# Issuing the keys' weight from ScalarE instead of SyncE at the start of a pre-LN linear-attention and feed-forward block

## The chip, the cores and the metric

The kernel runs on one core of one Trainium2 chip. The core has five engines with a queue of instructions each: TensorE (PE, whose weight loads are listed apart as PEld), VectorE (DVE), ScalarE (ACT), GpSimd (POOL) and SyncE (SP), which here only issues DMAs. Each engine takes its instructions in the order in which they stand in its queue. The DMAs are carried out by 16 DMA engines of the core. The metric is the device time in microseconds (us) of one execution.

## The reference

The inputs are bf16: x of 2048 rows by 512 columns, `wqkv` (512 by 1536), `wo` (512 by 512), `w1` (512 by 1792), `w2` (1792 by 512). Cut to what is computed:

```
ln = layernorm(x)
q, k, v = split(ln @ wqkv)                 # 32 heads of 16 columns
phi(t) = where(t > 0, t + 1, exp(t)) + 1e-6
kv = sum over rows of phi(k)^T v           # per head, 16 x 16
z  = sum over rows of phi(k)
o  = (phi(q) @ kv) / (phi(q) . z + 1e-6)
h  = x + o @ wo
out = h + relu(layernorm(h) @ w1) @ w2
```

## The kernel before

The 2048 rows are 16 tiles of 128 rows. Tile t holds, on partition p, row 16p + t, so tiles that follow each other lie side by side in DRAM on a partition: a DMA of one tile moves pieces of 1 KB, one of two tiles pieces of 2 KB, one of four tiles pieces of 4 KB. Four tiles make a chunk of 512 rows, and there are four chunks. All weights stay in SBUF. PSUM is used as eight banks of 512 columns (`bk`).

The work is written as small operations (`op_...`), and the string ORDER lists them in the order in which they are emitted; a word such as `K.0.3.0.2` calls `op_K(0, 3, 0, 2)`. Nothing reorders them afterwards, so ORDER fixes the order on each engine's queue. The waits between engines are semaphores that the framework adds by data dependence. For the DMAs it uses eight semaphores in turn (DMAHW0 to DMAHW7): the ninth DMA of the program waits until the first has landed, and so on.

The beginning of the program, for each tile t:

- `lx.t.n` (L201) loads n tiles of x into `x_nat`; `lk.k.n` (L204 and L206) loads n of the four row blocks of the keys' weight into `wk_sb` (two blocks are 256 KB). Both are issued by SyncE.
- `S.t` (L226, VectorE) takes the row statistics, `A.t` (L227, VectorE) turns them into mean and variance, `R.t.n` (L232 and L233, ScalarE) computes 1/sqrt by a Ln and an Exp, and `N.t` (L251, VectorE) writes the normalised tile into `h_nat`.
- `T.t` (L270, TensorE) transposes the normalised tiles 0 to 3 into PSUM, and `E.t` (L280, ScalarE) copies them out into `lnT`. The tiles from 4 on are transposed by DMA (`X.t`, L291, issued by SyncE).
- `K.t` (L299, TensorE) is the keys' projection of a tile, four matmuls of 512 columns with `wk_sb`. `F.t` (L317) and `U.t` (L320, both ScalarE) take exp and relu of it, `M.t` (L324) and `D.t` (L327, both VectorE) make phi(k) of the two.
- `G.t` (L351, TensorE) adds the tile's product of the normalised rows and phi(k) to the sum over rows, from which kv follows later.
- `table` (L166) loads ScalarE's function table, and `warm` (L215) runs 11 matmuls on zeros before the first data is there.

Behind these come the queries (`Q`, L307), the small products for kv, the division, the attention's output `h` (L494), the second layernorm, and the feed-forward part (`p`, L510, and `f`, L530), which takes the longer half of the time.

VectorE's queue begins, behind four memsets: S.0 S.1 A.0 S.2 A.1 S.3 A.2 N.0 A.3 N.1 N.2 N.3 S.4 S.5 A.4 A.5 S.7 N.5 S.6 M.0 A.7 A.6 D.0. The code of the loads:

```
    def op_lx(t, n):
        nc.sync.dma_start(out=x_nat[:, t : t + n, :], in_=x_v[:, t : t + n, :])

    op_lk = lambda k, n: load_d(wk_sb, wqkv_v[:, :, D : 2 * D], k, n)
```

Of the kernel before, what the change touches and what calls it, by code (L numbers as in the profile page):

```python
# [15 lines left out]


ORDER = """
const masks table lx.0.1 lx.1.1 lx.2.1 S.0 S.1 A.0 S.2 warm.1.6 lx.3.1 A.1 R.0.1 S.3 A.2 R.1.1 warm.9.6 N.0 A.3
N.1 R.2.1 R.3.1 lk.0.2 N.2 N.3 warm.1.6 T.0.2 T.1.7 lx.4.2 T.2.5 lk.2.2 S.4 E.0 S.5 T.3.4 A.4 K.0.3.0.2 E.1  # L20
K.1.0.0.2 lx.6.2 E.2 E.3 A.5 R.4.2 K.0.3.2.2 S.7 F.0.1 N.5 S.6 K.3.7 M.0.1 lx.8.4 K.2.2.0.2 U.0.1 lx.12.4 A.7
A.6 K.1.0.2.2 D.0.1 F.3.1 U.3.1 R.6.2 N.4 K.2.2.2.2 M.3.1 G.0 D.3.1 G.3 F.2.1 F.1.1 N.6 N.7 S.8 S.9 X.5 X.4
M.2.1 A.8 A.9 U.2.1 U.1.1 K.5.1 R.8.2 K.4.0 M.1.1 D.2.1 F.4.2 D.1.1 N.9 U.4.2 N.8 X.7 S.12 X.6 X.9 G.2 K.7.3
S.13 A.12 A.13 G.1 K.6.2 K.9.1 M.4.2 S.10 R.12.2 F.6.2 N.12 D.4.2 S.11 A.10 U.6.2 X.8 lq.0.2 M.6.2 N.13 G.4 X.12
K.8.0 A.11 R.10.2 D.6.2 lv.0.2 X.13 G.5 G.6 N.10 N.11 S.15 S.14 F.8.2 M.8.2 U.8.2 G.7 X.11 A.15 A.14 D.8.2
R.14.2 N.15 K.12.0 N.14 za.2 za.4 X.10 G.9 lq.2.2 lv.2.2 K.13.1 K.11.3 F.12.2 U.12.2 X.15 X.14 l2.10.4 l2.3.4
l1.0.2 K.10.2 G.8 M.12.2 F.10.2 U.10.2 za.6 D.12.2 M.10.2 za.8 D.10.2 Q.0.0.0 Q.0.1.1 qF.0.0.2 qU.0.0.2 za.10
qM.0.0.2 K.15.3 G.12 K.14.2 F.14.2 G.11 Q.0.2.0 Q.0.3.1 qF.0.2.2 G.13 za.12 M.14.2 W.14.2 zf.12 qD.0.0.2
qM.0.2.2 qU.0.2.2 G.10 G.14 z.3.3.14 G.15 z.1.3.14 z.2.3.14 z.0.3.14 qD.0.2.2 zc Q.1.0.2 gA.0.2 gA.2.2 zh dn.0.1
Q.1.1.3 dnl.0 kv.0.4 kv.2.4 kv.1.4 kv.3.4 lo.0.2 lo.2.2 dnx.0.2.2 qF.1.0.2 dnx.0.0.2 Q.1.2.0 rt.2.7 kx qM.1.0.2  # L30
Q.1.3.1 qF.1.2.2 m.0.4 m.1.5 rv.2 qW.1.0.2 qM.1.2.2 Q.3.1.7 m.3.6 Q.2.3.2 l1.2.2 dt.3 mA.0.2 qW.1.2.2 dt.0 dt.1
m.2.5 Q.2.1.4 dn.1.3 mA.2.2 dm.0.0.2 dm.0.2.2 dnl.1 dnx.1.2.2 Q.2.2.1 h.3.6 dnx.1.0.2 h.1.5 hD.3 dt.7 qF.2.2.2
rt.6.3 s.3 dt.4 re.6 h.0.0 hD.1 qU.2.2.2 dt.5 a.3 hD.0 s.1 s.0 qM.2.2.2 a.0 Q.3.0.6 h.2.5 Q.2.0.3 n.3 n.0 a.1
dm.1.0.2 Q.3.2.0 Q.3.3.1 dm.1.2.2 x.0 x.3 hD.2 n.1 s.2 qF.3.0.2 qU.2.0.2 qF.2.0.2 h.5.2 h.6.3 a.2 qU.3.0.2
qF.3.2.2 qM.2.0.2 h.4.7 n.2 qD.2.0.2 t.2.5 qD.2.2.2 hD.5 hD.4 h.7.4 dn.2.6 hD.7 e.2 dnl.2 x.1 hD.6 qM.3.0.2
p.0.0.5 dnx.2.2.2 p.0.13.7 p.0.1.6 p.0.8.2 p.0.11.4 qD.3.0.2 s.4 dnx.2.0.2 p.0.9.3 l2.7.3 dt.10 pA.0.0.2 dt.11
l2.0.3 dt.9 dt.8 p.0.12.6 qM.3.2.2 qW.3.2.2 s.6 pD.0.12.2 p.0.3.1 p.0.2.0 pA.0.8.2 s.7 r.0.4 dn.3.6 p.0.5.3
p.0.4.2 a.7 dm.2.0.2 dnl.3 pA.0.2.2 dnx.3.0.2 dnx.3.2.2 pA.0.4.2 dm.2.2.2 p.0.7.7 h.9.0 h.8.5 p.0.6.6 n.7 s.5
dt.13 dt.12 p.0.10.3 hD.9 hD.8 s.8 a.6 pD.0.6.2 dt.15 a.4 n.6 dt.14 pA.0.10.2 f.1.1.0.7 dm.3.0.2 dm.3.2.2 h.11.0
f.1.1.7.7 h.12.4 fo.1 s.9 h.15.6 h.14.5 h.10.3 f.0.2.0.7 a.8 a.9 a.5 hD.11 n.5 hD.12 x.6 hD.15 f.3.4.0.7 h.13.7  # L40
f.3.4.7.7 x.7 s.12 n.8 n.4 hD.14 f.0.2.7.7 x.4 x.5 p.1.0.6 f.2.5.0.7 s.11 s.14 hD.13 fo.3 fo.0 hD.10 a.11 s.10
n.9 p.1.5.3 p.1.1.7 s.15 a.12 pA.1.0.2 p.1.4.2 f.2.5.7.7 p.1.13.7 p.1.3.1 a.10 n.12 r.4.4 pA.1.4.2 p.1.2.0 n.11
p.1.8.4 fo.2 a.14 a.15 s.13 p.1.12.6 n.10 p.1.7.2 pD.1.2.2 n.14 p.1.6.1 x.11 p.1.9.5 pA.1.6.2 x.10 a.13 n.15 x.9
x.8 pD.1.8.2 fd.3 f.5.3.0.7 f.7.0.0.7 p.1.10.1 fd.1 fd.0 pA.1.12.2 p.1.11.2 pA.1.10.2 p.2.9.7 p.2.11.6 f.7.0.7.7
p.2.10.5 p.2.5.1 f.5.3.7.7 fo.7 pD.2.10.2 p.2.8.6 p.2.4.0 r.8.4 f.4.4.0.7 f.4.4.7.7 fo.5 p.2.0.2 pD.2.8.2
pD.2.4.2 p.2.1.3 x.12 n.13 p.2.3.6 p.2.2.5 fd.2 f.6.0.0.7 x.14 x.13 pA.2.0.2 pA.2.2.2 x.15 fo.4 p.3.3.7 p.3.7.1
p.3.2.6 p.3.9.5 p.3.8.4 f.6.0.7.7 pD.3.2.2 fo.6 pD.3.8.2 fd.4 p.3.11.7 p.3.4.2 p.3.10.6 p.3.5.3 p.3.6.0
pA.3.10.2 fd.7 pA.3.6.2 p.2.7.7 fd.5 fd.6 p.2.6.6 pA.2.6.2 p.3.13.5 pD.3.4.2 p.3.0.1 p.3.1.2 p.2.13.7 p.2.12.6
f.11.3.0.7 p.3.12.4 pA.3.0.2 pA.2.12.2 r.12.4 pD.3.12.2 f.9.6.0.7 f.14.2.0.7 f.10.7.0.7 f.11.3.7.7 f.10.7.7.7
f.9.6.7.7 f.8.1.0.7 f.12.5.0.7 f.8.1.7.7 f.13.0.0.7 f.15.4.0.14.3.1 f.14.2.7.7 fo.9 fo.10 fo.11 fd.10 fd.11 fd.9  # L50
f.12.5.7.7 fo.8 f.13.0.7.7 f.15.3.0.14.0.2 fd.8 fo.14 fo.12 fo.13 fo.15.3.1 fd.12 f.15.1.0.14.2.1 fd.13
fd.15.3.1 fd.14 fo.15.0.2 fd.15.0.2 fo.15.2.1 fd.15.2.1
"""
# [3 lines left out]
def kernel(  # L57
# [144 lines left out]

    def load_d(dst, src, k, n):
        nc.sync.dma_start(out=dst[:, k : k + n, :], in_=src[:, k : k + n, :])  # L204
# [376 lines left out]
```

## Time and profile before

| what | us |
|---|---|
| median of the runs before (170.41 to 173.28) | 170.55 |
| the profiled execution's own time | 170.57 |
| its span in the trace | 168.9 |
| TensorE busy in it | 162.5 |
| VectorE busy | 101.1 |
| ScalarE busy | 67.7 |

The span runs from the first to the last instruction that the trace shows; 1.7 us of the execution lie around it. "Busy" counts a matmul up to its modelled end, so TensorE at 96% isn't TensorE at its peak. In the timelines a row gives the start, the duration, engine, line, operation and what is written from what; a number in square brackets is the engine's idle time before it and what ended that. SPq is SyncE's queue: its rows are the issuing of a DMA, not the transfer.

### The profile page before, as it was taken

What the parts mean: (1) busy time and instruction counts of PE and PEld (TensorE: products, weight loads), DVE (VectorE), ACT (ScalarE), POOL (GpSimd) and SP (SyncE); (2) the same over time, 40 slices, a digit from 0 to 9 for tenths busy, and PEclk for the clock granted to TensorE, in tenths of its full rate; (3) what the DMA queues carried; (4) which work ended last, traced back from release to release, by engine and by line L of the source; (5) the groups of instructions that cost most, each with busy time, mean ns of one, the idle gap of its engine ahead of it and who ended that gap; (6) DMA issues with size and microseconds to landing.
All of it is one profiled execution on the core that took longest, in us unless ns stands there. A gap on an engine that the chain in (4) does not pass through costs nothing.

```text
span 168.9 us, 2311 instructions
## 1 busy us (share of the span) xinstructions
PE 162.5 (96%) x871; PEld 76.1 (45%) x871; DVE 101.1 (60%) x202; ACT 67.7 (40%) x100; POOL 4.7 (3%) x21
## 2 busy tenths in 40 slices
...
GB/s 124 276 240 92 89 178 117 217 385 336 37 64 62 64 157 67 151 62 97 33 64 0 31 36 157 86 4 0 80 76 0 31 4 0 0 0 88 36 35 93
DMA packets 30635, 15.49 MB, mean 92 GB/s; under 512 B 23200, under 2 KB 29600, under 8 KB 30624
## 3 DMA queue, kind: packets, MB, share of 16 engines
...
q8 instruction: 7, 0.11, 0.3%
...
HBM read 7.86 MB, written 2.10 MB: 59 GB/s over the span
## 4 chain that ended last, share of the span: by engine, by line
PE 91%; DMA 3%; SPq 2%; DVE 1%; issue 1%
PE bk L530 29%; PE bk L510 29%; PE bk L351 8%; PE bk L307 8%; PE bk L494 8%; PE bk L299 6%; DMA x_nat<-in_A_x_dram 3%; SPq L201 1%; PE bk L448 1%; PE bk L392 1%; SPq L204 1%; PE bk L404 1%; PE bk L270 0%; DVE st L226 0%; DVE pk_lo L327 0%
## 5 line engine op out<-in xcount | busy, mean ns | idle before, releaser
L530 PE MATMUL bk<-w_sb,at 128*128 128x512 bf16 (+2 forms) x252 | 50.7, 355 | 0.0
L510 PE MATMUL bk<-lnT,w_sb 128*128 128x512 bf16 x224 | 50.5, 379 | 0.0
L516 ACT ACTIVATE at<-bk 128x1024 bf16<-128x1024 f32 x17 | 17.3, 1021 | 55.6 <-PE bk L510 55.6
L530 PEld LDWEIGHTS <-at 128*128 128x128 bf16 x252 | 23.6, 98 | 25.2 <-DVE at L521 0.2
L510 PEld LDWEIGHTS <-w_sb 128*128 128x128 bf16 x224 | 21.8, 98 | 26.0
L538 DVE SCALAR_TENSOR_TENSOR gT<-bk,rstd,h_nat 128x512 bf16<-128x512 f32 (+2 forms) x18 | 12.2, 690 | 31.2 <-PE bk L530 31.2
L521 DVE TENSOR_SCALAR at<-bk 128x1024 bf16<-128x1024 f32 x11 | 13.3, 1220 | 20.7 <-PE bk L510 20.4
L317 ACT ACTIVATE eb<-bk 128x1024 bf16<-128x1024 f32 (+1 forms) x18 | 16.6, 926 | 6.7 <-PE bk L299 4.0
L307 PE MATMUL bk<-lnT,wq_sb 128*128 128x512 bf16 x64 | 15.8, 379 | 0.0
L299 PE MATMUL bk<-wk_sb,lnT 128*128 128x512 bf16 x64 | 15.3, 379 | 0.0
L494 PE MATMUL bk<-m_sb,pqs 128*128 128x512 bf16 x64 | 15.3, 379 | 0.0
L351 PE MATMUL bk<-at,h_nat 128*128 128x512 bf16 x56 | 13.6, 379 | 0.0
L320 ACT ACTIVATE rb<-bk 128x1024 bf16<-128x1024 f32 (+1 forms) x14 | 12.5, 903 | 0.7 <-PE bk L307 0.7
L226 DVE BATCH_NORM_STATS2 st<-x_nat 128x6 f32<-128x512 bf16 x16 | 10.5, 684 | 3.0 <-DMA x_nat<-in_A_x_dram 3.0
L500 DVE TENSOR_TENSOR h_nat<-bk,x_nat 128x512 bf16<-128x512 f32 x16 | 10.6, 681 | 2.4 <-PE bk L494 2.3
L228 DVE BATCH_NORM_STATS2 st<-h_nat 128x6 f32<-128x512 bf16 x16 | 10.8, 685 | 0.1
L351 PEld LDWEIGHTS <-h_nat 128*128 128x128 bf16 x64 | 6.2, 97 | 8.8 <-issue 1.8
L299 PEld LDWEIGHTS <-lnT 128*128 128x128 bf16 x64 | 5.9, 98 | 7.8 <-DMA lnT<-h_nat 1.4
L494 PEld LDWEIGHTS <-pqs 128*128 128x128 bf16 x64 | 6.1, 98 | 7.2 <-DVE pqs L484 0.8
L307 PEld LDWEIGHTS <-wq_sb 128*128 128x128 bf16 x64 | 5.9, 97 | 6.5 <-DMA wq_sb<-in_A_wqkv_dram 0.4
L461 ACT ACTIVATE wk_sb<-ld 128x1024 bf16<-128x1024 f32 x8 | 8.1, 1051 | 0.1
L324 DVE TENSOR_SCALAR eb<-eb 128x1024 bf16<-128x1024 bf16 (+1 forms) x18 | 6.9, 383 | 0.6 <-ACT eb L317 0.6
...
## 6 DMA issues: line engine op xcount, KB each, us to landing
out_dram<-gT SPq DMA_DIRECT2D x15, 128.0 KB, 1.9
...
x_nat<-in_A_x_dram SPq DMA_DIRECT2D x4, 128.0 KB, 2.5
wk_sb<-in_A_wqkv_dram SPq DMA_DIRECT2D x2, 256.0 KB, 4.2
x_nat<-in_A_x_dram SPq DMA_DIRECT2D x2, 256.0 KB, 5.0
```

The lines of the kernel that those rows point to most:

```text
L228: op_s = lambda t: nc.vector.bn_stats(out=st2[:, t, :], in_=h_nat[:, t, :])
L299: nc.tensor.matmul(bk[:, b, :], lhsT=lnT[c][:, kd, j * P : (j + 1) * P], rhs=wk_sb[:, kd, :], start=(kd == 0), stop=(kd == KD - 1),)
L307: nc.tensor.matmul(bk[:, b, :], lhsT=wq_sb[:, kd, j * P : (j + 1) * P], rhs=lnT[c][:, kd, :], start=(kd == 0), stop=(kd == KD - 1),)
L317: nc.scalar.activation(out=buf(eb, kind, i, n), in_=bank(at_bank[kind, i], n), func=ACT.Exp)
L320: nc.scalar.activation(out=buf(rb, kind, i, n), in_=bank(at_bank[kind, i], n), func=ACT.Relu)
L351: nc.tensor.matmul(bk[:, KD + kd, :], lhsT=ln_nat[:, t, kd * P : (kd + 1) * P], rhs=pk(t)[:, 0, :], start=(t == 0), stop=(t == NT - 1),)
L494: nc.tensor.matmul(bk[:, b, :], lhsT=pqs[:, (c * KD + jb) % NQ, j * P : (j + 1) * P], rhs=m_sb[:, jb, :], start=(jb == 0), stop=(jb == KD ...
L510: nc.tensor.matmul(bk[:, b, cols], lhsT=w1_sb[:, kd, f * P : (f + 1) * P], rhs=lnT[c][:, kd, cols], start=(kd == 0), stop=(kd == KD - 1),)
L516: nc.scalar.activation(out=acts[c % 2][:, f : f + n, :], in_=bank(at_bank["p", c, f], n), func=ACT.Relu)
L521: nc.vector.tensor_scalar(out=acts[c % 2][:, f : f + n, :], in0=bank(at_bank["p", c, f], n), scalar1=0.0, scalar2=None, op0=ALU.max,)
L530: nc.tensor.matmul(bk[:, b, 0 : w * P], lhsT=acts[c % 2][:, f, j * P : (j + 1) * P], rhs=w2_sb[:, f, k * P : (k + w) * P], start=(f == 0), ...
L538: nc.vector.scalar_tensor_tensor(out=o_t[:, t % NO, cols], in0=bk[:, at_bank["f", t, k], 0 : w * P], scalar=rstd2[:, t : t + 1], in1=h_nat ...
```

## The change

The two loads of the keys' weight are issued by ScalarE's queue, as its first two instructions, ahead of the table load. SyncE issues only x at the start, and tiles 2 and 3, which were two DMAs of 128 KB, become one of 256 KB. The order of all other operations stays. In ORDER, four words `lx.0.1 lx.1.1 lx.2.1 lx.3.1` become `lx.0.1 lx.1.1 lx.2.2`, the words `lk.0.2` and `lk.2.2` go, `la.0.2 la.2.2` come, and all words `lx` stand at the front.

```diff
 ORDER = """
-const masks table lx.0.1 lx.1.1 lx.2.1 S.0 S.1 A.0 S.2 warm.1.6 lx.3.1 A.1 R.0.1 S.3 A.2 R.1.1 warm.9.6 N.0 A.3
-N.1 R.2.1 R.3.1 lk.0.2 N.2 N.3 warm.1.6 T.0.2 T.1.7 lx.4.2 T.2.5 lk.2.2 S.4 E.0 S.5 T.3.4 A.4 K.0.3.0.2 E.1
...
+const masks la.0.2 la.2.2 table lx.0.1 lx.1.1 lx.2.2 lx.4.2 lx.6.2 lx.8.4 lx.12.4 S.0 S.1 A.0 S.2 warm.1.6 A.1
...
+    def op_la(k, n):
+        nc.scalar.dma_start(out=wk_sb[:, k : k + n, :], in_=wqkv_v[:, k : k + n, D : 2 * D])
```

(A second new function, `op_xa`, would load x by ScalarE; no word of ORDER calls it.)

On SyncE, the start of the queue before, with the semaphores that a row waits for; 128x512 is one tile of x, 128x1024 two, 128x2048 four, and `wk_sb` is the keys' weight:

```order
L201 DMA x_nat<-in_A_x_dram 128x512 x4
L204 DMA wk_sb<-in_A_wqkv_dram 128x2x512
L201 DMA x_nat<-in_A_x_dram 128x1024
L204 DMA wk_sb<-in_A_wqkv_dram 128x2x512
L201 DMA x_nat<-in_A_x_dram 128x1024
L201 DMA x_nat<-in_A_x_dram 128x2048 [waits DMAHW0_49]
L201 DMA x_nat<-in_A_x_dram 128x2048 [waits DMAHW1_49]
L291 DMA_TRANSPOSE lnT_82<-h_nat 128x4x128 [waits DMAHW2_49,DVE_49]
```

The same place now (line numbers behind L204 are 6 higher, since two functions are added):

```order
L201 DMA x_nat<-in_A_x_dram 128x512 x2
L201 DMA x_nat<-in_A_x_dram 128x1024 x3
L201 DMA x_nat<-in_A_x_dram 128x2048
L201 DMA x_nat<-in_A_x_dram 128x2048 [waits DMAHW0_49]
L297 DMA_TRANSPOSE lnT_82<-h_nat 128x4x128 [waits DMAHW1_49,DVE_49]
```

Three instructions are gone from SyncE's queue: the two of the weight, and one by joining tiles 2 and 3. DMAHW0 is now the semaphore of the weight's first half, which is the program's first DMA, so the load of tiles 12 to 15 waits for that, where before it waited for tile 1; the first DMA transpose waits for the weight's second half where it waited for tile 2.

On ScalarE, the start of the queue before, from the branch into the program on:

```order
L576 UNCONDITIONAL_BRANCH [waits barrier_Pool_Activation_PE_DVE_SP_release]
L166 ACT_TABLE_LOAD
L232 ACTIVATE rstd<-mv,eps_73 128x1 [waits DVE_49]
L233 ACTIVATE rstd<-rstd 128x1 [waits Activation_49]
L232 ACTIVATE rstd<-mv,eps_73 128x1 [waits DVE_49]
```

And now:

```order
L582 UNCONDITIONAL_BRANCH [waits barrier_Pool_Activation_PE_DVE_SP_release]
L210 DMA wk_sb<-in_A_wqkv_dram 128x2x512 x2
L166 ACT_TABLE_LOAD
L238 ACTIVATE rstd<-mv,eps_73 128x1 [waits DVE_49]
L239 ACTIVATE rstd<-rstd 128x1 [waits Activation_49]
```

Two DMA issues stand ahead of the table load and wait for nothing. TensorE's, VectorE's and GpSimd's queues hold the same rows in the same order as before.

More of the change, by code (lines that the diff above doesn't have):

```diff
@@ L18 @@
 ORDER = """
-const masks table lx.0.1 lx.1.1 lx.2.1 S.0 S.1 A.0 S.2 warm.1.6 lx.3.1 A.1 R.0.1 S.3 A.2 R.1.1 warm.9.6 N.0 A.3
-N.1 R.2.1 R.3.1 lk.0.2 N.2 N.3 warm.1.6 T.0.2 T.1.7 lx.4.2 T.2.5 lk.2.2 S.4 E.0 S.5 T.3.4 A.4 K.0.3.0.2 E.1
-K.1.0.0.2 lx.6.2 E.2 E.3 A.5 R.4.2 K.0.3.2.2 S.7 F.0.1 N.5 S.6 K.3.7 M.0.1 lx.8.4 K.2.2.0.2 U.0.1 lx.12.4 A.7
-A.6 K.1.0.2.2 D.0.1 F.3.1 U.3.1 R.6.2 N.4 K.2.2.2.2 M.3.1 G.0 D.3.1 G.3 F.2.1 F.1.1 N.6 N.7 S.8 S.9 X.5 X.4
-M.2.1 A.8 A.9 U.2.1 U.1.1 K.5.1 R.8.2 K.4.0 M.1.1 D.2.1 F.4.2 D.1.1 N.9 U.4.2 N.8 X.7 S.12 X.6 X.9 G.2 K.7.3
@@ L24 @@
[L24 to L48, printed above, removed]
@@ L49 @@
-f.11.3.0.7 p.3.12.4 pA.3.0.2 pA.2.12.2 r.12.4 pD.3.12.2 f.9.6.0.7 f.14.2.0.7 f.10.7.0.7 f.11.3.7.7 f.10.7.7.7
-f.9.6.7.7 f.8.1.0.7 f.12.5.0.7 f.8.1.7.7 f.13.0.0.7 f.15.4.0.14.3.1 f.14.2.7.7 fo.9 fo.10 fo.11 fd.10 fd.11 fd.9
+const masks la.0.2 la.2.2 table lx.0.1 lx.1.1 lx.2.2 lx.4.2 lx.6.2 lx.8.4 lx.12.4 S.0 S.1 A.0 S.2 warm.1.6 A.1
+R.0.1 S.3 A.2 R.1.1 warm.9.6 N.0 A.3 N.1 R.2.1 R.3.1 N.2 N.3 warm.1.6 T.0.2 T.1.7 T.2.5 S.4 E.0 S.5 T.3.4 A.4
+K.0.3.0.2 E.1 K.1.0.0.2 E.2 E.3 A.5 R.4.2 K.0.3.2.2 S.7 F.0.1 N.5 S.6 K.3.7 M.0.1 K.2.2.0.2 U.0.1 A.7 A.6
@@ new lines @@
+K.1.0.2.2 D.0.1 F.3.1 U.3.1 R.6.2 N.4 K.2.2.2.2 M.3.1 G.0 D.3.1 G.3 F.2.1 F.1.1 N.6 N.7 S.8 S.9 X.5 X.4 M.2.1
+A.8 A.9 U.2.1 U.1.1 K.5.1 R.8.2 K.4.0 M.1.1 D.2.1 F.4.2 D.1.1 N.9 U.4.2 N.8 X.7 S.12 X.6 X.9 G.2 K.7.3 S.13 A.12
+A.13 G.1 K.6.2 K.9.1 M.4.2 S.10 R.12.2 F.6.2 N.12 D.4.2 S.11 A.10 U.6.2 X.8 lq.0.2 M.6.2 N.13 G.4 X.12 K.8.0
+A.11 R.10.2 D.6.2 lv.0.2 X.13 G.5 G.6 N.10 N.11 S.15 S.14 F.8.2 M.8.2 U.8.2 G.7 X.11 A.15 A.14 D.8.2 R.14.2 N.15
+K.12.0 N.14 za.2 za.4 X.10 G.9 lq.2.2 lv.2.2 K.13.1 K.11.3 F.12.2 U.12.2 X.15 X.14 l2.10.4 l2.3.4 l1.0.2 K.10.2
@@ new lines @@
+G.8 M.12.2 F.10.2 U.10.2 za.6 D.12.2 M.10.2 za.8 D.10.2 Q.0.0.0 Q.0.1.1 qF.0.0.2 qU.0.0.2 za.10 qM.0.0.2 K.15.3
+G.12 K.14.2 F.14.2 G.11 Q.0.2.0 Q.0.3.1 qF.0.2.2 G.13 za.12 M.14.2 W.14.2 zf.12 qD.0.0.2 qM.0.2.2 qU.0.2.2 G.10
+G.14 z.3.3.14 G.15 z.1.3.14 z.2.3.14 z.0.3.14 qD.0.2.2 zc Q.1.0.2 gA.0.2 gA.2.2 zh dn.0.1 Q.1.1.3 dnl.0 kv.0.4
+kv.2.4 kv.1.4 kv.3.4 lo.0.2 lo.2.2 dnx.0.2.2 qF.1.0.2 dnx.0.0.2 Q.1.2.0 rt.2.7 kx qM.1.0.2 Q.1.3.1 qF.1.2.2
+m.0.4 m.1.5 rv.2 qW.1.0.2 qM.1.2.2 Q.3.1.7 m.3.6 Q.2.3.2 l1.2.2 dt.3 mA.0.2 qW.1.2.2 dt.0 dt.1 m.2.5 Q.2.1.4
@@ new lines @@
+dn.1.3 mA.2.2 dm.0.0.2 dm.0.2.2 dnl.1 dnx.1.2.2 Q.2.2.1 h.3.6 dnx.1.0.2 h.1.5 hD.3 dt.7 qF.2.2.2 rt.6.3 s.3 dt.4
+re.6 h.0.0 hD.1 qU.2.2.2 dt.5 a.3 hD.0 s.1 s.0 qM.2.2.2 a.0 Q.3.0.6 h.2.5 Q.2.0.3 n.3 n.0 a.1 dm.1.0.2 Q.3.2.0
+Q.3.3.1 dm.1.2.2 x.0 x.3 hD.2 n.1 s.2 qF.3.0.2 qU.2.0.2 qF.2.0.2 h.5.2 h.6.3 a.2 qU.3.0.2 qF.3.2.2 qM.2.0.2
+h.4.7 n.2 qD.2.0.2 t.2.5 qD.2.2.2 hD.5 hD.4 h.7.4 dn.2.6 hD.7 e.2 dnl.2 x.1 hD.6 qM.3.0.2 p.0.0.5 dnx.2.2.2
+p.0.13.7 p.0.1.6 p.0.8.2 p.0.11.4 qD.3.0.2 s.4 dnx.2.0.2 p.0.9.3 l2.7.3 dt.10 pA.0.0.2 dt.11 l2.0.3 dt.9 dt.8
```

16 lines of the change are left out of this document (added).

## The prediction

> **What bounds the kernel now.** I read the page first (busy shares, then the chain that ended last), then TensorE's waits, then the chain's first 13 us, and last the timelines and transfers there.
>
> ```profile
> span 168.9 us, 2311 instructions
> PE 162.5 (96%) x871; PEld 76.1 (45%) x871; DVE 101.1 (60%) x202; ACT 67.7 (40%) x100; POOL 4.7 (3%) x21
> ...
> PE 91%; DMA 3%; SPq 2%; DVE 1%; issue 1%
> ```
>
> The kernel is TensorE from end to end: 91% of the chain is matmuls. The change touches none of them. What it can touch is the time in which TensorE waits, and TensorE's list of waits has only three entries:
>
> ```profile
> PE bk L215 <- DVE ones L177: 1.3, 1, 1.3
> PE bk L270 <- DVE h_nat L251: 1.2, 1, 1.2
> PE bk L351 <- DVE pk_lo L327: 1.0, 1, 1.0
> ```
>
> The columns are the total, the number of times and the longest. All three lie in the first 13 us: the start, T.0 waiting for N.0, and G.0 waiting for D.0. Behind G.0 TensorE has no wait in the list, so whatever G.0 moves by, the end moves by. The chain shows what set G.0:
>
> ```profile
> 4.12 5.80 DMA x_nat<-in_A_x_dram
> ...
> 9.95 0.04 DVE st L226
> ...
> 10.56 0.40 DVE h_nat L251
> 10.96 0.60 DVE st L226
> ...
> 11.86 0.44 DVE pk_lo L327
> ...
> 12.33 0.81 PE bk L351 x3
> ```
>
> The load of tiles 6 and 7, issued at 4.12, lands at 9.92; S.7 starts at 9.95, and N.5, S.6, M.0 and D.0 follow on VectorE without a break until G.0 at 12.33. VectorE's timeline up to there:
>
> ```profile
> 3.08 1.30 DVE L226 BATCH_NORM_STATS2 st<-x_nat 128x6 f32<-128x512 bf16 x2 [1.86 <-DMA x_nat<-in_A_x_dram]
> ...
> 4.39 0.66 DVE L226 BATCH_NORM_STATS2 st<-x_nat 128x6 f32<-128x512 bf16 x1
> ...
> 5.16 0.69 DVE L226 BATCH_NORM_STATS2 st<-x_nat 128x6 f32<-128x512 bf16 x1
> ...
> 5.85 0.45 DVE L251 TENSOR_SCALAR h_nat<-x_nat,mv,rstd 128x512 bf16<-128x512 bf16 x1
> ...
> 7.32 1.28 DVE L226 BATCH_NORM_STATS2 st<-x_nat 128x6 f32<-128x512 bf16 x2
> 8.51 0.30 DVE L227 BATCH_NORM_AGGREGATE mv<-st 128x2 f32<-128x6 f32 x2
> 9.95 0.69 DVE L226 BATCH_NORM_STATS2 st<-x_nat 128x6 f32<-128x512 bf16 x1 [1.14 <-DMA x_nat<-in_A_x_dram]
> ```
>
> From S.0 at 3.08 on VectorE works through S.1, S.2 (4.39), S.3 (5.16), N.0 (5.85), S.4 and S.5 (7.32), A.4 and A.5 (8.51 to 8.81), and only then stands still for 1.14 us, for tiles 6 and 7. So there is a **cushion of 1.14 us**: VectorE could run 1.14 us late up to 8.81 and G.0 would still start at 12.33.
>
> **What the change does.** SyncE's part of it, as it is now:
>
> ```profile
> 0.80 1.82 SPq L201 DMA_DIRECT2D x_nat<-in_A_x_dram  x4
> 2.66 0.43 SPq L204 DMA_DIRECT2D wk_sb<-in_A_wqkv_dram  x1
> 3.14 0.47 SPq L201 DMA_DIRECT2D x_nat<-in_A_x_dram  x1
> 3.65 0.43 SPq L204 DMA_DIRECT2D wk_sb<-in_A_wqkv_dram  x1
> 4.12 1.42 SPq L201 DMA_DIRECT2D x_nat<-in_A_x_dram  x3
> ```
>
> *Removed:* three issues from SyncE, 0.43 us each and 0.05 between. x is issued at 0.80, 1.26, 1.72 (tiles 2 and 3), 2.2 (4 and 5) and 2.7 (6 and 7) instead of 0.80 to 2.19, 3.14 and 4.12. Tiles 6 and 7 thus go out 1.4 us earlier. That is worth something only if the transfers, not the issuing, have room:
>
> ```profile
> 2.00:4.00 2.00, 2.00 (x6) 0.76 (x5) 0.92 (x2) 0.08 (x1) 1.72 (x7) 1.00 0.98 240
> 4.00:6.00 2.00, 1.16 (x5) 0.29 (x3) 1.97 (x7) 1.03 (x5) 1.65 (x7) 1.00 0.83 227
> 6.00:8.00 2.00, 1.64 (x18) 1.04 (x19) 2.00 (x7) 1.94 (x7) 0.15 (x1) 1.00 1.02 302
> 8.00:10.00 2.00, 2.00 (x11) 0.89 (x10) 0.86 (x5) 1.97 (x6) 0.00 (x0) 1.00 0.92 353
> ```
>
> The last two columns are the mean busy share of the 16 DMA engines and GB/s. From 2 to 10 us the engines are busy 0.83 to 1.02 of the time: they are already full, with one queue feeding them. And what has to pass before tiles 6 and 7 are in is the same in both orders: all of tiles 0 to 7 (1024 KB) and the weight (512 KB). So I expect their landing near 9.9 as before, at most some 0.3 earlier. The earlier issue buys nearly nothing.
>
> *Moved:* the weight's 512 KB. Before, it stood behind tiles 0 to 3; now its issue starts at about 0.8 on ScalarE, beside tile 0. What was landed when, in KB counted from the first DMA, comes from the transfers' view, one row for each DMA (KB, us from issue to landing); the issues are, in this order, tile 3 (2.19), the weight's first half (2.66), tiles 4 and 5 (3.14) and the weight's second half (3.65):
>
> ```profile
> x_nat<-in_A_x_dram SPq DMA_DIRECT2D x1, 128.0 KB, 2.9
> ...
> wk_sb<-in_A_wqkv_dram SPq DMA_DIRECT2D x1, 256.0 KB, 3.9
> ...
> x_nat<-in_A_x_dram SPq DMA_DIRECT2D x1, 256.0 KB, 4.1
> ...
> wk_sb<-in_A_wqkv_dram SPq DMA_DIRECT2D x1, 256.0 KB, 4.6
> ```
>
> Tile 3 landed at 5.1 as KB 512, the first half at 6.6 as KB 768, tiles 4 and 5 at 7.2 as KB 1024, the second half at 8.2 as KB 1280. I use this as a clock for any order of the same transfers. Issue to landing of tiles 2 and 3 under two queues is not in this trace, so it is bounded: not before 5.1 if the weight took no bandwidth from x (KB 512, as now), and 7.2 if all of the weight passes first (KB 1024). Between them I take an estimate: if the DMA engines take turns row by row between the two queues, then when the last of tile 0's 128 rows, tile 1's 128 and the 128 double rows of tiles 2 and 3 is through, 384 of the weight's 512 rows are too: 512 + 384 = KB 896, about **6.9**, midway between 6.6 and 7.2. By the same count tile 0 lands at KB 256 and tile 1 at KB 512 (5.1), so S.0 and S.1 are late as well but done by 5.9, under the wait of S.2.
>
> The Trainium skill, "DMA: Bandwidth & Descriptors", section "Issuing engines are not separate DMA queues", speaks against this change: DMAs that several engines start run on the same 16 DMA engines and interleave, and only issue time on the sequencer is saved. By it the sum stands as taken; were it wrong, the lower bound would hold. No row of this trace shows two queues at once.
>
> *The sum.* S.3 now starts at 5.16 and N.0 at 5.85. S.2 to S.3 is 5.16 - 4.39 = 0.77, some of it the wait for tile 3; S.0 to S.1, where nothing waits, is 1.30 - 0.69 = 0.61; with A.1 between I take 0.7. With S.2 at 6.9, S.3 starts at 7.6. VectorE is thus late by 7.6 - 5.16 = 2.4 us up to A.5, which ends at 11.2, behind the landing of tiles 6 and 7: the wait of 1.14 is gone. S.7, and with it G.0, is late by 2.4 - 1.14 = **1.3 us**. With the bounds 6.6 and 7.2 it is 1.0 and 1.6.
>
> TensorE in that stretch:
>
> ```profile
> 6.36 1.49 PE L270 MATMUL bk<-ident,h_nat 128*128 128x128 bf16 x16 [1.20 <-DVE h_nat L251]
> 7.69 3.62 PE L299 MATMUL bk<-wk_sb,lnT 128*128 128x512 bf16 x16
> ```
>
> The transposes and the K matmuls are late by the whole 2.4 us: K ends at 7.69 + 3.62 + 2.4 = 13.7, and D.0 allows G.0 at 12.33 + 1.3 = 13.6. The two meet; at most 0.1 is added, and since successive matmuls overlap at their ends I count 0.
>
> *Added:* two DMA issues ahead of the table load.
>
> ```profile
> 0.79 1.28 ACT L166 ACT_TABLE_LOAD   x1 [0.79 <-PEq L565]
> 4.50 0.29 ACT L232 ACTIVATE rstd<-mv,eps 128x1 f32<-128x1 f32 x1 [2.43 <-DVE mv L227]
> ```
>
> At SyncE's 0.43 + 0.05 each, the load ends at 3.0 instead of 2.07, and R.0 isn't due before 4.50, later still now: ScalarE's idle 2.43 us hides it, and the cost is 0 (if the cover went, 0.95). *Landing of the weight:* K.0, due at 7.69 + 2.4, needs its first half, there by about 7.2 at the latest by the clock above: hidden. *The new semaphore waits:* the load of tiles 12 to 15 now waits for the weight's first half, until up to 7.2 instead of 5.1; ahead of it 512 KB of tiles 8 to 11 keep the DMA engines fed meanwhile, so nothing. The first transpose waits for the second half, long landed when N.5 allows it.
>
> So 170.57 (the profiled execution, span 168.9 and 1.7 around it, equal to the median of 170.55 within 0.02) + 1.3 = **171.9 us**, 0.8% slower.
>
> **Rivals.**
>
> *Neutral: x keeps its place.* If tile 0 to 3's loads hold their lead (ScalarE's DMAs start moving later, or its queue gets less), VectorE is late by up to 1.14 us only, and tiles 6 and 7 decide as they do now: 170.3 to 170.9. For it: SyncE's 1.72 for tiles 2 and 3 isn't later than now. Against: the weight is issued as early as tile 0, and the engines are full.
>
> *Faster: two queues move more.* The engines move 240 GB/s at 2 to 4 us and 353 at 8 to 10, at like busy shares, so the early rate, on 1 KB rows, isn't their ceiling. If two queues bring the late rate forward, tiles 2 and 3 come at 4.5 to 5, tiles 6 and 7 before 8.81, and the third of TensorE's waits, 1.0 us, falls: 169.5 to 170.3, no better, as the 1.2 us wait for N.0 stays. Against: the busy share.
>
> *Slower still: TensorE falls back to its slow pace.*
>
> ```profile
> 1.25 3.91 PE L215 MATMUL bk<-m_sb 128*128 128x512 bf16 x11 [1.25 <-DVE ones L177]
> ...
> 2.51 0.15 PEld L215 LDWEIGHTS <-m_sb 128*128 128x128 bf16 x1 [0.28 <-issue]
> ...
> 2.93 0.15 PEld L215 LDWEIGHTS <-m_sb 128*128 128x128 bf16 x1 [0.28 <-issue]
> ...
> 4.13 0.53 PEld L215 LDWEIGHTS <-m_sb 128*128 128x128 bf16 x3 [0.19 <-issue]
> ```
>
> The first warm matmuls' weights are loaded 2.93 - 2.51 = 0.42 us apart; from 4.13 on three fit into 0.53, and the K matmuls take 3.62 / 16 = 0.23 each. So TensorE is slow for its first 4.13 - 1.25 = 2.9 us, though the windows give the granted clock as 1.00 there too. The idle between warm and T.0, 1.20 us now, becomes 1.20 + 2.4 = 3.6 us. If that much idle brings the slow pace back, each K matmul costs 0.2 more: 0.8 us for the four or so that fall into the first 2.9 us of work from T.0 on (T itself takes 1.3 of them), 3.2 us for all 16, and G.0 takes all of it, as TensorE and VectorE meet there: 172.7 to 175.1. It decides from an idle that is longer than this trace's 1.2 us, and it passes 2% if over ten of the K matmuls are slow. For it: the slow start. Against: the idle is short, and T's matmuls end it.
>
> The Trainium skill, "TensorE: Matmul & The Clock Gate", section "What's actually happening", has the gate go back to half rate after an idle window of about 3.4 us that runs freely; by it a gap of 3.6 us need not contain a whole window, and the time would be the forecast's or this rival's as the window happens to fall.
>
> **How the numbers follow.** The forecast has 0.58, its own range 171.1 to 172.6 (bounds 6.6 and 7.2, and some 0.4 for the slowest of the 16 engines); neutral 0.15, faster 0.10, slow pace 0.15, and 0.02 for anything else. The range leaves out the faster case and the dearer half of the slow pace: 170.2 to 173.4. Over 2% slower (above 173.96) is the dear third of the slow pace, 0.05; over 2% faster, below 167.1, is out of reach of the 1.0 us wait, 0.01; within 2%, about what a measurement of this kernel can tell from no change, 0.94.
>
> **What would show it.** S.2's row on VectorE with a wait for x of about 1 us and a start near 6.9; tiles 2 and 3 with some 5.2 us from issue to landing; N.0 near 8.3; the idle before T.0 at 3.6; no idle before S.7; G.0 near 13.6; K matmuls still 0.23 each; ScalarE's table load ending near 3.0. I am wrong if S.2 starts before 5.8, if S.7 still waits for x, or if the K matmuls take 0.42 each.

## The result and the profile after

The changed kernel takes 172.38 us (median, 171.37 to 172.74) against 170.55: the ratio is 1.0113, with a 95% interval of 1.0073 to 1.0152. That is 1.1% slower, and inside the forecast range (170.2 to 173.4), 0.5 us above the forecast of 171.9. The profiled execution took 172.74, with a span of 171.0, 2.2 us longer than the span before. Executions over 1.5% above the fastest of their kernel (173.28 and 172.29 of the kernel before, 172.69 of e9_before_warm below) are left out of the ratios. Lines behind L204 are 6 higher now: L226 is L232, L299 is L305, L351 is L357.

TensorE's waits, which had three entries, have two; the columns are the total, the number and the longest:

```profile
PE bk L276 <- DVE h_nat L257: 2.7, 1, 2.7
PE bk L221 <- DVE ones L177: 1.2, 1, 1.2
```

T.0's wait for N.0 has grown from 1.2 to 2.7 us, and the wait of G.0 is gone. VectorE's timeline shows where T.0's wait comes from:

```profile
3.32 0.70 DVE L232 BATCH_NORM_STATS2 st<-x_nat 128x6 f32<-128x512 bf16 x1 [2.10 <-DMA x_nat<-in_A_x_dram]
4.59 0.69 DVE L232 BATCH_NORM_STATS2 st<-x_nat 128x6 f32<-128x512 bf16 x1 [0.57 <-DMA x_nat<-in_A_x_dram]
...
6.76 0.69 DVE L232 BATCH_NORM_STATS2 st<-x_nat 128x6 f32<-128x512 bf16 x1 [1.40 <-DMA x_nat<-in_A_x_dram]
...
8.12 0.38 DVE L257 TENSOR_SCALAR h_nat<-x_nat,mv,rstd 128x512 bf16<-128x512 bf16 x1
...
10.96 0.66 DVE L232 BATCH_NORM_STATS2 st<-x_nat 128x6 f32<-128x512 bf16 x1
```

S.0, S.1 and S.2 each wait for x now (3.08, 3.69 and 4.39 before, the last two without a wait). S.2 starts at 6.76, N.0 at 8.12 instead of 5.85, and S.7 at 10.96 without a wait. The transfers' view of the two DMAs that matter (KB, us to landing), tiles 2 and 3 issued at 1.72, tiles 6 and 7 at 2.66:

```profile
x_nat<-in_A_x_dram SPq DMA_DIRECT2D x1, 256.0 KB, 5.0
...
x_nat<-in_A_x_dram SPq DMA_DIRECT2D x1, 256.0 KB, 5.8
```

Tiles 2 and 3 land at 6.7, tiles 6 and 7 at 8.5. TensorE's timeline, and the windows from 8 to 14 us (granted clock, DMA share and GB/s are the last three columns):

```profile
1.25 4.61 PE L221 MATMUL bk<-m_sb 128*128 128x512 bf16 x11 [1.25 <-DVE ones L177]
8.55 1.85 PE L276 MATMUL bk<-ident,h_nat 128*128 128x128 bf16 x16 [2.70 <-DVE h_nat L257]
10.20 4.65 PE L305 MATMUL bk<-wk_sb,lnT 128*128 128x512 bf16 x16
14.68 1.03 PE L357 MATMUL bk<-pk_lo,h_nat 128*128 128x512 bf16 x4
```

```profile
8.00:10.00 2.00, 1.45 (x15) 1.29 (x16) 1.99 (x8) 1.81 (x7) 0.00 (x0) 0.72 0.87 353
10.00:12.00 2.00, 2.00 (x9) 0.88 (x8) 1.98 (x7) 1.57 (x5) 0.00 (x0) 0.50 0.06 25
12.00:14.00 2.00, 2.00 (x10) 0.84 (x9) 1.26 (x6) 1.27 (x3) 0.00 (x0) 0.93 0.32 63
```

The clock falls to 0.5 during the transposes T and stays there while the first five K matmuls run: the 16 take 4.65 us instead of 3.62, 1.03 more, and K starts 1.65 behind T.0's start instead of 1.33, 0.32 more. G.0 starts at 14.68 instead of 12.33, 2.35 late, and the span ends 2.2 late. The rows add up to that: T.0 starts 2.19 late, T and K lose 0.32 and 1.03 to the pace, and against this stand the 1.03 of idle that was ahead of G.0 before and 0.17 by which G.0 now starts ahead of K's modelled end. Without the pace, 2.19 - 1.03 - 0.17, about 1.0, would be left in this execution. The chain says the same; these are pieces of it up to G.0 (start, duration, what):

```profile
1.72 5.02 DMA x_nat<-in_A_x_dram
...
6.76 0.69 DVE st L232
...
8.55 1.85 PE bk L276 x16
10.40 4.44 PE bk L305 x16
14.85 1.29 PE bk L357 x6
```

It leads over tiles 2 and 3, not over tiles 6 and 7, and from T.0 on it stays on TensorE.

So two things seem to add up: a late landing, near 1.0 here, and a slow pace of TensorE, near 1.35. The experiments separate them, and part the late landing into the weight's lead and the joining of tiles 2 and 3.

### The profile page after: what moved, and what is told of

It reads as the page before. It is cut to its first block, busy times and chain, and to the rows that moved or that the text cites. A ratio compares the mean times of both kernels' runs of the same rounds, so it can differ in the third digit from the quotient of the medians.

```text
span 171.0 us, 2310 instructions
## 1 busy us (share of the span) xinstructions
PE 164.2 (96%) x871; PEld 77.2 (45%) x871; DVE 101.4 (59%) x202; ACT 67.8 (40%) x100; POOL 4.8 (3%) x21
## 4 chain that ended last, share of the span: by engine, by line
PE 88%; DMA 4%; DVE 3%; ACT 1%; SPq 1%; issue 0%
PE bk L536 28%; PE bk L516 28%; PE bk L313 8%; PE bk L500 8%; PE bk L305 6%; PE bk L357 6%; DMA x_nat<-in_A_x_dram 3%; PE bk L276 1%; DMA lnT<-h_nat 1%; DVE st L232 1%; PE bk L454 1%; DVE h_nat L257 1%; ACT eb L323 1%; ACT rb L326 1%; PE bk L398 1%; PE bk L410 1%
## 5 line engine op out<-in xcount | busy, mean ns | idle before, releaser
L305 PE MATMUL bk<-wk_sb,lnT 128*128 128x512 bf16 x64 | 16.5, 398 | 0.1
L357 PE MATMUL bk<-at,h_nat 128*128 128x512 bf16 x56 | 13.7, 379 | 0.0
L232 DVE BATCH_NORM_STATS2 st<-x_nat 128x6 f32<-128x512 bf16 x16 | 10.6, 683 | 4.1 <-DMA x_nat<-in_A_x_dram 4.1
L305 PEld LDWEIGHTS <-lnT 128*128 128x128 bf16 x64 | 6.3, 102 | 8.8 <-DMA lnT<-h_nat 1.6
L357 PEld LDWEIGHTS <-h_nat 128*128 128x128 bf16 x64 | 6.2, 98 | 7.3
```

The source lines that it names most:

```text
L232: op_S = lambda t: nc.vector.bn_stats(out=st[:, t, :], in_=x_nat[:, t, :])
L305: nc.tensor.matmul(bk[:, b, :], lhsT=lnT[c][:, kd, j * P : (j + 1) * P], rhs=wk_sb[:, kd, :], start=(kd == 0), stop=(kd == KD - 1),)
L357: nc.tensor.matmul(bk[:, KD + kd, :], lhsT=ln_nat[:, t, kd * P : (kd + 1) * P], rhs=pk(t)[:, 0, :], start=(t == 0), stop=(t == NT - 1),)
```

## The experiments

Each was compared with executions of the kernel before on the same chip. Its median was 170.55 beside the changed kernel, 170.52 beside e1 to e4, 170.38 beside e5 to e8 and 170.32 beside e9 to e11; these last three groups ran on three different chips, so medians of different groups are best compared by what each adds to its own.

| kernel | edit | median us | ratio to before, 95% interval |
|---|---|---|---|
| the changed kernel | | 172.38 | 1.0113 (1.0073 to 1.0152) |
| e8_after_again | none | 172.36 | 1.0121 (1.0081 to 1.0161) |
| e1_warm | + 12 warm matmuls | 171.46 | 1.0064 (1.0043 to 1.0085) |
| e2_split23 | tiles 2, 3 apart | 172.02 | 1.0114 (1.0061 to 1.0167) |
| e10_lead_warm | tiles 2, 3 apart, + 6 warm | 170.90 | 1.0037 (1.0012 to 1.0063) |
| e4_join_only | before, tiles 2, 3 joined | 170.99 | 1.0022 (0.9988 to 1.0056) |
| e11_join_warm | the same, + 9 warm | 170.80 | 1.0025 (0.9999 to 1.0051) |
| e9_before_warm | before, + 5 warm | 170.50 | 1.0013 (0.9984 to 1.0041) |
| e3_after_table | weight's DMAs behind the table load | 172.28 | 1.0128 (1.0075 to 1.0180) |
| e5_hold | weight's DMAs held until 2.3 us | 170.01 | 0.9983 (0.9957 to 1.0010) |
| e6_hold_split | the same, tiles 2, 3 apart, + 3 warm | 169.79 | 0.9967 (0.9943 to 0.9991) |
| e7_sync_front | weight first, on SyncE | 173.60 | 1.0200 (1.0150 to 1.0251) |

### The slow pace taken away

```diff
-... N.2 N.3 warm.1.6 T.0.2 ...
+... N.2 N.3 warm.13.6 T.0.2 ...
```

> The changed kernel with 12 more matmuls on zeros behind the warm ones, so that TensorE works through most of the 2.7 us in which it now waits for N.0. Theory (two causes: tiles 2 and 3 land 2.3 us late, of which the cushion takes 1.14, and the idle brings TensorE's slow pace back, which costs about 1.1): the granted clock stays at 1.00 from 8 to 12 us, K takes 0.23 each, G.0 starts near 13.5 instead of 14.7, and the profiled execution comes to 171.4 to 171.9. Rival (the late landing alone made the loss, the slow pace was covered): G.0 stays near 14.7 and the time at 172.4 to 172.7.

171.46, all ten executions between 171.35 and 171.97. In the profile tiles 2 and 3 land at 6.3, and TensorE's timeline and windows read, with N.0 and N.5 on VectorE behind them:

```profile
4.64 4.08 PE L221 MATMUL bk<-m_sb 128*128 128x512 bf16 x15
8.55 1.11 PE L276 MATMUL bk<-ident,h_nat 128*128 128x128 bf16 x16
9.63 3.80 PE L305 MATMUL bk<-wk_sb,lnT 128*128 128x512 bf16 x16
13.27 1.02 PE L357 MATMUL bk<-pk_lo,h_nat 128*128 128x512 bf16 x4
```

```profile
8.00:10.00 2.00, 2.00 (x22) 1.20 (x20) 2.00 (x7) 1.72 (x7) 0.00 (x0) 1.00 0.73 295
10.00:12.00 2.00, 2.00 (x11) 0.74 (x10) 1.72 (x6) 1.97 (x7) 0.00 (x0) 1.00 0.01 4
```

```profile
7.70 0.38 DVE L257 TENSOR_SCALAR h_nat<-x_nat,mv,rstd 128x512 bf16<-128x512 bf16 x1
...
11.48 0.41 DVE L257 TENSOR_SCALAR h_nat<-x_nat,mv,rstd 128x512 bf16<-128x512 bf16 x1 [0.28 <-ACT rstd L239]
```

The clock stays at 1.00, K takes 0.24 each, G.0 starts at 13.27. Twelve matmuls on zeros, work that nothing needs, make the kernel 0.9 us faster. The rival that the slow pace was covered falls. What stays is 171.46 - 170.52 = 0.94; in the profiles G.0 is 13.27 - 12.33 = 0.94 late and the executions are 0.81 apart (171.38 against 170.57). Most of that is the late landing, but not all: the twelve were a few too many. N.0 was done at 8.08, the added matmuls held TensorE until T.0 at 8.55, and N.5 then waited 0.28 for ScalarE, which first had to copy T's results out. S.7 started at 10.54, only 0.59 late. So, by these rows, the landing's share in this execution lies between 0.6 and 0.9.

### The changed kernel again

> The changed kernel once more, without an edit, for its spread. Theory (the late landing costs 0.8 to 1.3 in every execution and the slow pace about 1.1 more in those in which it comes): executions with a mean granted clock of 1.0 lie near 171.4, those with 0.99 near 172.4, with nothing between tied to anything else; a profile has either both or only the late landing. Rival (one cause): the times do not split by the clock.

172.36. The expectation was too simple: the six times don't split by the mean clock. Five executions have 0.99 and 171.9 to 172.4; the sixth, the profiled one, has 1.0 and yet 173.55. Its timeline:

```profile
8.25 1.89 PE L276 MATMUL bk<-ident,h_nat 128*128 128x128 bf16 x16 [2.13 <-DVE h_nat L257]
9.93 5.64 PE L305 MATMUL bk<-wk_sb,lnT 128*128 128x512 bf16 x16
15.41 1.03 PE L357 MATMUL bk<-pk_lo,h_nat 128*128 128x512 bf16 x4
```

K takes 5.64 us. Two of TensorE's weight loads for K show when the pace changes:

```profile
13.77 0.15 PEld L305 LDWEIGHTS <-lnT 128*128 128x128 bf16 x1 [0.28 <-issue]
14.12 0.96 PEld L305 LDWEIGHTS <-lnT 128*128 128x128 bf16 x5 [0.19 <-issue]
```

Up to 13.77 they are 0.43 apart, from 14.12 on five fit into 0.96: TensorE hadn't left its first slow pace before 14 us. The profiles of e3_after_table and e7_sync_front below show the same, up to 14.0 and 14.1. The trace holds no record of the clock in that execution, and the profile then prints 1.00. So the pace is to be read from the matmuls' times, and the mean clock of 1.0 means either "always fast" or "no change recorded". By the times and the clock, none of these six executions seems to have been free of the slow pace; of the four behind the result one came to 171.37, with a clock of 1.0, near e1_warm's time.

### Tiles 2 and 3 apart

```diff
-const masks la.0.2 la.2.2 table lx.0.1 lx.1.1 lx.2.2 lx.4.2 ...
+const masks la.0.2 la.2.2 table lx.0.1 lx.1.1 lx.2.1 lx.3.1 lx.4.2 ...
```

> The changed kernel with tiles 2 and 3 loaded by two DMAs of 128 KB, as before the change; the weight still issued first by ScalarE. Theory (the weight ahead of x is what delays S.2 and S.3, the joining only makes S.2 wait for tile 3 as well): tile 2 lands near 5.9 and tile 3 near 6.8, S.3 starts near 6.8 instead of 7.46, VectorE is late by 1.7 instead of 2.3, and the time falls by about 0.6 against the changed kernel, to 171.7 or so. Rival (the joining is the cause): tiles 2 and 3 land near 4.3 and 5.2 as before, S.3 starts near 5.2, and the time is at or below 170.6.

The profile has S.2 at 5.64 and N.0 at 6.99, 1.14 late, between theory and rival, and just what the cushion holds:

```profile
5.64 0.69 DVE L232 BATCH_NORM_STATS2 st<-x_nat 128x6 f32<-128x512 bf16 x1 [0.35 <-DMA x_nat<-in_A_x_dram]
...
6.99 0.38 DVE L257 TENSOR_SCALAR h_nat<-x_nat,mv,rstd 128x512 bf16<-128x512 bf16 x1
```

```profile
7.43 1.53 PE L276 MATMUL bk<-ident,h_nat 128*128 128x128 bf16 x16 [1.31 <-DVE h_nat L257]
8.80 3.62 PE L305 MATMUL bk<-wk_sb,lnT 128*128 128x512 bf16 x16
12.31 1.02 PE L357 MATMUL bk<-pk_lo,h_nat 128*128 128x512 bf16 x4
```

G.0 is at 12.31, where it was before, and this execution took 170.47. But the other four took 171.81 to 172.49, three of them with a clock of 0.99, so the median of 172.02 says little of the landing: the slow pace covers it. That asked for the same comparison with the pace held.

### Four kernels with the pace held

e9_before_warm: `warm.1.6 T.0.2` becomes `warm.6.6 T.0.2` in the kernel before. e10_lead_warm: the same place becomes `warm.7.6` in e2_split23. e11_join_warm: `warm.10.6` in e4_join_only, which is the kernel before with

```diff
-const masks table lx.0.1 lx.1.1 lx.2.1 S.0 S.1 A.0 S.2 warm.1.6 lx.3.1 A.1 ...
+const masks table lx.0.1 lx.1.1 lx.2.2 S.0 S.1 A.0 S.2 warm.1.6 A.1 ...
```

> The kernel before with only tiles 2 and 3 joined in one DMA; the weight stays on SyncE in its old places. Theory: the joined tiles land near 5.1, when tile 3 did, S.2 waits for them and S.3 starts near 5.8, 0.6 late; the cushion of 1.14 takes it, and tiles 6 and 7, issued 0.5 earlier, still decide S.7 near 9.5 to 9.9: 170.2 to 170.7. Rival (the joining alone costs): 171.2 or more.

> The kernel before with 5 more warm matmuls on zeros, which fill its 1.2 us before T.0; nothing else. It is the base for the next two, in which the same is done, so that the three differ in the late landing alone. Theory: the slow pace hardly ever comes in the kernel before, T.0 moves by 0.3 at most: 170.0 to 170.7. Rival (the kernel before is slowed in part of its executions too): 169.7 or less in the median, with a narrower spread than the kernel before.

> The weight issued first by ScalarE, tiles 2 and 3 in two DMAs, and 6 more warm matmuls, so that the slow pace stays away. Theory (the lead alone makes S.3 about 1.2 late, which the cushion of 1.14 takes): G.0 near 12.3, 170.4 to 170.8, equal to the kernel before; with the changed kernel plus warm matmuls at 171.46, the joining then costs 0.7 to 1.0 on top of the lead. Rival (the lead alone is the cost): 171.2 to 171.5.

> The kernel before with tiles 2 and 3 joined and 9 more warm matmuls. Theory (the joining alone makes S.3 about 1.2 late, which the cushion takes; what the joining cost without the warm matmuls was the slow pace): G.0 at 12.0 to 12.5, 170.0 to 170.6, with a spread under 1. Rival (the joining alone costs): 171 or more.

With the pace held: neither 170.50, the joining alone 170.80, the lead alone 170.90, both (e1_warm) 171.46. Over the kernel before, each on its own chip, these are 0.18, 0.48, 0.58 and 0.94. Each alone thus costs some 0.3 to 0.4 over neither, a little more than I expected for the two (170.0 to 170.6 and 170.4 to 170.8); the interval of the joining alone still touches 1, that of the lead alone doesn't. Together they cost 0.94 - 0.18 = 0.76, about the sum of the two; whether they add up exactly isn't shown, since e1_warm and e9_before_warm also carry matmuls that run on past N.0 (in e9_before_warm T.0 starts at 6.70, N.0 ends at 6.31). Neither delay was wholly taken by the cushion: in the profiles N.0 was 1.33 late with the joining and 1.69 with the lead, and G.0 came at 12.49 and 12.86. The kernel before isn't helped by warm matmuls (1.0013, interval over 1), and one of the ten executions with them took 172.69 at a clock of 0.99, so they don't keep every slow stretch away.

e4_join_only without warm matmuls is instructive by its spread, 169.96 to 171.55; its median of 170.99 is above the expected 170.2 to 170.7. Its profiled execution (171.55) had tiles 2 and 3 at 5.6, not near 5.1, and N.0 1.2 late, about what the cushion holds: S.7 started at 9.88, no later than the 9.95 before. It lost the time to the pace; S.2 on VectorE, then T.0 and K on TensorE, then two of the windows:

```profile
5.69 0.69 DVE L226 BATCH_NORM_STATS2 st<-x_nat 128x6 f32<-128x512 bf16 x1 [0.92 <-DMA x_nat<-in_A_x_dram]
```

```profile
7.48 1.85 PE L270 MATMUL bk<-ident,h_nat 128*128 128x128 bf16 x16 [2.18 <-DVE h_nat L251]
9.12 4.62 PE L299 MATMUL bk<-wk_sb,lnT 128*128 128x512 bf16 x16
```

```profile
6.00:8.00 2.00, 0.52 (x6) 0.36 (x7) 2.00 (x8) 1.28 (x6) 0.15 (x1) 0.93 1.00 320
8.00:10.00 2.00, 2.00 (x15) 1.45 (x14) 1.99 (x7) 2.00 (x6) 0.00 (x0) 0.50 0.98 389
```

After an idle of 2.18 us the clock fell; after 1.20 and 1.31 us (the kernel before and e2_split23's profile) K kept its 3.62 us.

e9_before_warm shows something about the cushion itself. It loads in the order of the kernel before, with tiles 6 and 7 issued at 4.12; the transfers' row of these, and TensorE's of G.0:

```profile
x_nat<-in_A_x_dram SPq DMA_DIRECT2D x1, 256.0 KB, 4.5
```

```profile
11.42 1.02 PE L351 MATMUL bk<-pk_lo,h_nat 128*128 128x512 bf16 x4
```

The tiles took 4.5 us, not 5.8, landed at 8.6, S.7 didn't wait, and G.0 came at 11.42; this execution took 169.59. So the cushion of 1.14 us belongs to one execution. The kernel before itself ranges from 169.5 to 171.4, with two executions at 172.29 and 173.28, and a landing that varies by 1.3 us can account for a good part of the range up to 171.4; how much of it was not shown.

### ScalarE's queue, or the lead?

```diff
-const masks la.0.2 la.2.2 table lx.0.1 ...
+const masks table la.0.2 la.2.2 lx.0.1 ...
```

> The changed kernel with ScalarE's two loads of the weight behind its table load instead of ahead, so that they are issued near 2.1 and 2.6 us. Theory (only the weight's lead over tiles 0 to 3 costs; issuing x early from SyncE helps tiles 6 and 7, which landed at 8.5 in the changed kernel): tiles 0 and 1 land at 3.1 and 3.7 as before, tiles 2 and 3 at 5.0 to 5.6, VectorE is late by less than its cushion of 1.14, tiles 6 and 7 land before 9, G.0 starts at 11.4 to 12.2, and the time is 169.6 to 170.4. Rival (a second queue delays x whenever it runs, by its bytes): tiles 2 and 3 near 6.5, 171.5 or more.

172.28, as the changed kernel: the edit didn't do what I meant. ScalarE's timeline:

```profile
0.79 1.28 ACT L166 ACT_TABLE_LOAD   x1 [0.79 <-PEq L571]
0.82 0.98 ACTq L210 DMA_DIRECT2D wk_sb<-in_A_wqkv_dram  x2
```

The two DMAs are issued from 0.82 on, while the load ahead of them in the queue runs until 2.07. The weight had its lead as before; tiles 2 and 3 landed at 6.4. To delay a DMA it has to wait for something:

```diff
+    def op_hold():
+        nc.scalar.activation(out=wk_sb[:, 0, 0:1], in_=eps5[:], func=ACT.Copy)
...
-const masks la.0.2 la.2.2 table lx.0.1 ...
+const masks table hold la.0.2 la.2.2 lx.0.1 ...
```

> The changed kernel with the table load first and one small ScalarE instruction behind it (it writes one column of the weight's tile, which the load then overwrites), so that the two loads of the weight, still on ScalarE, wait for it and are issued near 2.3 and 2.8 us. Theory (the weight's lead over tiles 0 to 3 costs, not ScalarE's queue): tiles 0 and 1 land near 3.3 and 3.8, tiles 2 and 3 at 5.2 to 5.8, VectorE is late by 0.7 to 1.3, which the cushion takes, tiles 6 and 7 land by 9; 170.0 to 170.6 where the granted clock stays at 1.00, 171.5 where the idle before T.0 brings the slow pace. Rival (a second queue takes bandwidth from x whenever it runs): tiles 2 and 3 at 6.3 to 6.7, 171.5 to 172.5 in most executions.

170.01, ten executions from 169.83 to 171.07. ScalarE's rows, then S.2's on VectorE (lines 9 higher than in the kernel before):

```profile
2.09 0.21 ACT L210 ACTIVATE wk_sb<-eps 128x1 bf16<-128x1 f32 x1
2.33 0.96 ACTq L213 DMA_DIRECT2D wk_sb<-in_A_wqkv_dram  x2
```

```profile
5.08 0.69 DVE L235 BATCH_NORM_STATS2 st<-x_nat 128x6 f32<-128x512 bf16 x1 [0.68 <-DMA x_nat<-in_A_x_dram]
```

With 1.5 us less lead, from the same queue, tiles 2 and 3 land at 5.1, T.0 waits 0.74, and the loss of 1.8 us is gone. The rival, that a second queue takes from x whenever it runs, falls. The other way round, the lead without ScalarE:

```diff
-const masks la.0.2 la.2.2 table lx.0.1 ...
+const masks table lk.0.2 lk.2.2 lx.0.1 ...
```

> The two loads of the weight issued by SyncE as its first two DMAs, ahead of all of x; ScalarE issues none, tiles 2 and 3 joined. Theory (it is the weight's bytes ahead of x, whichever engine issues them): tiles 2 and 3 land near 7.0 to 7.4, as KB 1024, S.2 starts there, G.0 is at least as late as in the changed kernel, 14.7 or more where the slow pace comes, and the time is 172.3 to 173.2. Rival (two queues at once are what slows x): tiles 2 and 3 land before 6.3, and the time is 171.5 or less.

173.60, the slowest of all, 0.4 beyond the theory's 173.2. Tiles 2 and 3 landed at 6.9, and the profile has the slow pace up to 14.1 on top. VectorE's first row, and TensorE's K matmuls:

```profile
5.88 1.29 DVE L232 BATCH_NORM_STATS2 st<-x_nat 128x6 f32<-128x512 bf16 x2 [4.66 <-DMA x_nat<-in_A_x_dram]
```

```profile
10.60 5.34 PE L305 MATMUL bk<-wk_sb,lnT 128*128 128x512 bf16 x16
```

Here even tile 0 waits behind the whole weight, until 5.9. What costs is the weight's bytes ahead of x, whichever engine sends them.

### A version that beats both

e5_hold with `lx.2.1 lx.3.1` for `lx.2.2` and `warm.4.6` ahead of T.0:

> The same, with tiles 2 and 3 in two DMAs again and three more warm matmuls. Theory (no lead of the weight, no wait of S.2 for tile 3, SyncE's x issued early): tiles 2 and 3 land at 4.3 and 5.2 to 5.8, VectorE is late by 0 to 0.6, tiles 6 and 7 land before 8.8, S.7 waits for nothing, G.0 starts at 11.3 to 12.0, and the time is 169.5 to 170.2, below the kernel before by 0.3 to 1.0. Rival: no better than the kernel before, 170.5 or more.

169.79, ratio 0.9967 (0.9943 to 0.9991). TensorE's waits and timeline (T, the first four K matmuls, the other twelve, G.0):

```profile
PE bk L224 <- DVE ones L177: 1.2, 1, 1.2
PE bk L308 <- DMA wk_sb<-in_A_wqkv_dram: 0.3, 1, 0.3
PE bk L308 <- DMA lnT<-h_nat: 0.2, 1, 0.2
```

```profile
6.15 1.53 PE L279 MATMUL bk<-ident,h_nat 128*128 128x128 bf16 x16
7.51 1.03 PE L308 MATMUL bk<-wk_sb,lnT 128*128 128x512 bf16 x4
8.81 2.75 PE L308 MATMUL bk<-wk_sb,lnT 128*128 128x512 bf16 x12 [0.27 <-DMA wk_sb<-in_A_wqkv_dram]
11.44 1.02 PE L360 MATMUL bk<-pk_lo,h_nat 128*128 128x512 bf16 x4
```

The gain is 0.3%. G.0 is 0.9 earlier than in the profile of before, though no earlier than in e9_before_warm's (11.42): what the edit changes over ten executions is the spread, 169.47 to 170.46 against 169.59 to 172.69. Which of its three parts (the held weight, the separate tiles, the warm matmuls) brings this wasn't tested one by one. Two new waits take part of it: K's second half for its weight, 0.3, hidden ahead of G.0, and later, at 26 us, a K matmul for a transposed tile, 0.2.

## Why the prediction held, and where it didn't

**The late landing: right in mechanism, a little too large.** Tiles 2 and 3 were put at 6.9, the measured landings of the changed kernel are 6.7 and, in e8_after_again's profile, 6.4; S.3 2.4 us late, measured 2.3 (7.46 against 5.16); the wait before S.7 gone, as said; TensorE and VectorE meeting at G.0, as said, where the pace is held: in e1_warm D.0 ends at 13.22 and K's last matmul at 13.43 by the model, with G.0 at 13.27 (in the changed kernel's own profile the slow K matmuls decide, and D.0 waits for them). The term was 1.3 us; S.7 is 1.0 late in the changed kernel's profile, 0.7 in e8_after_again's and 0.6 in e1_warm's, and the time with the pace held is 0.94 up.

The estimate of 6.9 was off in two ways that partly cancel: the whole weight passed before tiles 2 and 3 (its second half landed at 6.0), where the taking of turns row by row had three quarters of it, which by the KB clock would have given 7.2; and the KB clock ran at the old order's rate, where the changed kernel moved more (see below). The 0.4 that the range adds "for the slowest of the 16 engines" has no row of before behind it; the landings of tiles 2 and 3 in the three executions of these loads are 6.7, 6.4 and 6.3. The Trainium skill's rule ("DMA: Bandwidth & Descriptors", "Issuing engines are not separate DMA queues"), that DMAs of several engines interleave on the same 16 DMA engines, agrees with this: tile 1 landed at 4.6 instead of 3.7 with the weight beside it.

**The slow pace: the step that failed.** It stood as a rival with a chance of 0.15, so the sum left it out, and it comes in nearly every execution of the changed kernel. One of the signs of being wrong that the prediction named, K matmuls of 0.42 each, is there for five of the 16. The argument against it, "the idle is short, and T's matmuls end it", was wrong on both counts: 2.70 us of idle were enough in the changed kernel, 2.18 in e4_join_only, and behind T the first five K matmuls were slow. (The idle was forecast at 3.6; N.0 came 2.27 late, but the warm matmuls also ended 0.70 later.) Its price, 0.8 us for "the four or so" matmuls, came out near, 1.03 on K, 0.32 on T and 0.9 in the time, but by another count: by the windows the slow stretch is 3.4 us from 8.9 on, not the first 2.9 us from T.0. Without the pace the forecast of 171.9 would have been 0.4 too high; with it, it was 0.5 too low. The two errors partly cancel: that the total lay where it was forecast is in part luck, since the reason given was half of the real one.

**Tiles 6 and 7 "near 9.9, at most some 0.3 earlier": wrong, without consequence.** They landed at 8.5 in the changed kernel. "They are already full" overlooked that a busy share near 1 doesn't fix the GB/s: the windows of the changed kernel move 274, 302 and 346 GB/s from 2 to 8 us, where the kernel before moves 240, 227 and 302. But e9_before_warm had them at 8.6 in the old order, so the old order's 9.9 was one execution's. Since VectorE reached S.7 only at 10.96, neither mattered. To this extent the faster rival was right, more was moved, and the bytes that came early were the weight's. That the second queue did it is likely but not shown: e7_sync_front, with the same loads on one queue, moved 280, 226 and 344, in one execution.

**Costs put at nothing: right.** The table load ended at 3.10, R.0 started at 5.40; K.0's weight landed at 4.1 and 6.0, before 10.20; the load of tiles 12 to 15, which waited for the weight's first half, was issued at 4.1 and landed before it was needed. And G.0's shift goes through to the end: 2.35 at G.0, 2.2 in the span.
